# Experts of a mixture-of-experts stage: the smallest one moves from last to third, a 32-slot group becomes 32 extra columns, another group is finished after the last tile

## The chip, the cores and the metric

The kernel runs on one core of a Trainium2 chip. The metric is the device time of one execution in microseconds (us), as the median of several runs. The engines are TensorE (PE for matmuls, PEld for its weight loads), VectorE (DVE), ScalarE (ACT), GpSimd (POOL) and SyncE (SP). Here SP issues the loads of the weights, and POOL issues the indirect transfers that gather rows of tokens from the output tensor and scatter results back.

## The reference, cut to what matters

```python
def _attn_ref(q, k, v, centroids):                 # 4 batches, 8 heads, 768 tokens, 64 wide
    q_assign = argmax(q_n . c_n); k_assign = argmax(k_n . c_n)      # 16 clusters per head
    scores = where(q_assign == k_assign, q . k / 8, -1e9)
    return softmax(scores) . v

def _moe_ref(x, w_skip, w_gate, w1, w2):           # x: 3072 tokens of 512; 8 experts, 1024 hidden
    do_compute = x @ w_skip > 0
    e_idx, gate_w = argmax and softmax weight of (x @ w_gate)
    for e in range(E):
        h = maximum(x[mask] @ w1[e], 0.0)
        y[mask] = gate_w[mask, None] * (h @ w2[e])
    out[do_compute] = x + y                        # the other tokens keep x
```

## The kernel before, in words

The attention takes the first 440 us or so and writes x to the output tensor; the expert stage, which the change touches, works on that tensor in place. Expert 0 is computed beside the end of the attention. The seven others stand at positions p = 1 to 7 of the loop at the end of `experts` (from L1711). Position 1 is the fullest expert known before the last batch, and positions 2 to 7 are the rest by falling number of tokens; `positions` finds which expert that is, at run time. `SHAPE[p]` says how many slots a position has: so many tiles of 128 tokens, and groups of 32 for what goes beyond. Before: position 1 has 256 slots, position 2 has 256 + 32 (group 0, the far group), position 3 has 128 + 64 (groups 1, 2), positions 4 to 6 have 128 + 32 (groups 3, 4, 5), position 7 has 128.

Products are made of float32 numbers split into a high and a low part (`split` for weights, `turned` for rows, which are transposed on TensorE first), three matmuls for each (`three`). There are three ways through an expert:

- A full expert (256 slots): `hidden` keeps the weights as stationary operand and moves 256 columns of tokens, 96 matmuls; `result` then does the second layer for each tile of 128 tokens, 24 matmuls of 512 columns each.
- A light expert (128 slots): `hidden_rows` moves 512 columns of weights, 24 matmuls; its result goes to SBUF (`HS`), is transposed and split (`turn`), and `second_layer` is 24 more.
- A group of 32 slots: it works in plain float32 on the unsplit weights. `group_turn` transposes its rows, `group_hidden` (L1636) makes 16 matmuls of 256 columns, `group_back` (L1646) transposes the result with two, `group_result` (L1655) makes 32 matmuls of 128 columns. `group_hidden` and `group_back` run one position ahead of `group_result`, which stands at the head of its own position.

All results end in `mix` (L1178, x + gate * y, DVE) and `scatter` (L1328, POOL). `gather` is L1321. A scatter writes the output tensor that a gather reads, so a gather that is queued behind scatters waits for them to land, and a scatter behind gathers waits for those. POOL takes its queue in order. `gathers(p + 2)` fetches the rows of the position after the next one, `group_gathers` those of the groups; the places of the groups come from `group_lists` (far group) and `group_places` (others), both in position 1.

The weights come in pieces of 512 KB through eight buffers (`wraw`); `ahead` asks for the next four, and a piece can be loaded once the buffer's old piece has been split and, where a group reads it, used by `group_hidden` or `group_result`. The split (L1552 on ACT for the high part, L1553 on DVE for the low part) goes into one set of tiles for w1 and one for w2, so the split for p + 1 trails the last matmuls of p.

The order of instructions on each engine comes from the framework's scheduler, which starts from the order of the code; `overflow_table` (DVE, a table for tokens beyond all slots; the loop at the very end runs zero times on this input) is spread between other work.

## Time and profile before

| | |
|---|---|
| median of 3 runs (lowest, highest) | 596.77 us (596.75, 597.57) |
| the profiled execution: its own time | 597.92 us |
| its span, first to last instruction | 596.2 us |
| PE busy | 578.9 us (97%) |
| DVE, ACT, POOL busy | 486.9 (82%), 390.6 (66%), 358.6 (60%) us |
| last matmul ends at | 587.8 us |

The times of the trace are microseconds from the start of the span. Positions 1 to 7 run from about 452 us to the end. In the timeline a row gives the start, the duration, the engine and line, what is written from what, how many instructions were merged into the row, and in square brackets how long the engine was idle before it and what released it. A plain float32 matmul leaves two records.

### The profile page before, as it was taken

The page shows a single profiled execution, that of the slowest core. Times are in us where ns is not written, and L with a number is a line of the kernel's source. Part 1 is how long each engine was busy: PE and PEld are TensorE (multiplying, and loading weights), DVE is VectorE, ACT ScalarE, POOL GpSimd, SP SyncE. Part 2 cuts the span into 40 slices and gives each one's busy share as a digit, 9 for nine tenths or more (in the row PEclk, how much of TensorE's full clock was granted, in tenths as well). Part 3 has the DMA queues.
Part 4 walks back from the last instruction along what each step waited for, and adds up shares of the span by engine and source line. Part 5 has one row for each costly group of instructions (what it writes and reads, how often), then busy time and mean ns, then how long its engine had stood idle before and what let it go on. Part 6 is the DMA issues. An engine that isn't in the chain of part 4 may idle for free.

```text
span 596.2 us, 12896 instructions
## 1 busy us (share of the span) xinstructions
PE 578.9 (97%) x4118; PEld 416.6 (70%) x4118; DVE 486.9 (82%) x1032; ACT 390.6 (66%) x917; POOL 358.6 (60%) x391
## 2 busy tenths in 40 slices
PE   7899999999999999999999999999999999999994
PEld 2566667777677766777676776665589787777773
DVE  7987698897989997899997897888569985666781
ACT  7467768677767875778667775975346525566670
POOL 8976859688868877688867686753023230323210
PEclk9999999999999999999999999999999999999998
DMA  7396696766856876668676694765133694598730
GB/s 221 85 235 145 168 216 151 172 152 170 197 140 169 205 177 163 159 154 205 165 159 164 183 221 113 220 185 167 30 125 126 235 320 142 201 305 292 269 123 19
DMA packets 52517, 105.05 MB, mean 176 GB/s; under 512 B 8395, under 2 KB 22777, under 8 KB 52448
## 3 DMA queue, kind: packets, MB, share of 16 engines
q1 hardware_dynamic: 49904, 97.81, 60.7%
q0 software_dynamic: 2144, 6.19, 2.9%
q8 instruction: 34, 0.56, 0.4%
q14 instruction: 35, 0.29, 0.2%
q10 hardware_dynamic: 400, 0.20, 0.1%
HBM read 55.76 MB, written 9.57 MB: 110 GB/s over the span
## 4 chain that ended last, share of the span: by engine, by line
PE 84%; DVE 6%; issue 4%; DMA 2%; POOL 1%; ACT 1%; SPq 1%; POOLq 0%; ACTq 0%; DVEq 0%
PE ps L718 21%; PE ps L692 12%; PE ps L633 11%; PE ps L693 11%; PE ps L1139 4%; PE ps L1140 4%; PE ps L1141 4%; PE ps L748 2%; PE ps L538 2%; PE ps L807 2%; PE ps L1158 2%; PE ps L1655 2%; PE ps L1161 2%; PE ps L1162 2%; PE ps L1636 2%
## 5 line engine op out<-in xcount | busy, mean ns | idle before, releaser
L635 DVE TENSOR_REDUCE M<-ps 128x1 f32<-128x512 f32 (+1 forms) x374 | 190.9, 551 | 41.8 <-PE ps L633 38.3
L707 POOL TENSOR_TENSOR acc<-acc,PT 128x384 f32<-128x384 f32 x134 | 123.5, 950 | 42.9 <-ACT PT L695 39.7
L692 PE MATMUL ps<-D 98*128 98x384 f32 x384 | 134.9, 351 | 2.6 <-DVE M L635 2.4
L707 POOL TENSOR_TENSOR acc<-acc,wraw 128x384 f32<-128x384 f32 x112 | 112.0, 1031 | 31.4 <-ACT wraw L695 25.9
L633 PE MATMUL ps<-D 96*128 96x512 f32 (+1 forms) x374 | 129.0, 348 | 1.8 <-ACT D L600 1.7
L693 PE MATMUL ps<-D 128*128 128x384 f32 x384 | 130.0, 339 | 0.0
L695 ACT ACTIVATE PT<-ps 128x384 f32<-128x384 f32 x216 | 98.7, 495 | 39.4 <-PE ps L693 32.7
L695 ACT ACTIVATE wraw<-ps 128x384 f32<-128x384 f32 x168 | 77.9, 494 | 16.0 <-PE ps L693 6.5
L692 PEld LDWEIGHTS ps<-D 98*128 98x128 f32 x384 | 72.8, 190 | 19.7 <-issue 6.4
L633 PEld LDWEIGHTS ps<-D 96*128 96x128 f32 x374 | 70.7, 190 | 13.8 <-issue 5.8
L693 PEld LDWEIGHTS ps<-D 128*128 128x128 f32 x384 | 73.1, 190 | 7.5
L718 PE MATMUL ps<-PT,vt 128*64 128x385 f32 x432 | 75.4, 492 | 0.0
L718 PE MATMUL ps<-wraw,vt 128*64 128x385 f32 x336 | 57.9, 492 | 0.0
L718 PEld LDWEIGHTS ps<-PT,vt 128*64 128x64 f32 x432 | 28.8, 136 | 34.8 <-issue 33.9
L1552 ACT ACTIVATE D<-wraw 128x1024 fp32r<-128x1024 f32 (+1 forms) x45 | 43.9, 1009 | 8.8 <-PE ps L1141 7.0
L1328 POOL DMA_INDIRECT out<-yo,ixw x7 | 11.1, 1583 | 54.9 <-DVE yo L1178 49.2
L718 PEld LDWEIGHTS ps<-wraw,vt 128*64 128x64 f32 x336 | 22.7, 137 | 27.4 <-issue 26.1
L489 DVE TENSOR_TENSOR raw<-raw,D 128x768 fp32r<-128x768 f32 x28 | 41.7, 1501 | 0.0
L701 POOL TENSOR_TENSOR acc<-PT 128x384 f32<-128x384 f32 x36 | 30.7, 872 | 14.6 <-ACT PT L695 14.5
L1553 DVE TENSOR_TENSOR D<-wraw,D 128x1024 fp32r<-128x1024 f32 (+1 forms) x29 | 33.9, 1182 | 5.5 <-ACT D L1552 5.4
L829 ACT ACTIVATE x<-ps,rs 128x64 f32<-128x64 f32 x162 | 35.3, 307 | 2.7 <-DVE rs L760 1.2
L701 POOL TENSOR_TENSOR acc<-wraw 128x384 f32<-128x384 f32 x28 | 28.0, 1020 | 5.9 <-ACT wraw L695 5.9
(377 smaller groups left out, 1033.6 us busy)
## 6 DMA issues: line engine op xcount, KB each, us to landing
wraw<-w SPq DMA_DIRECT2D x64, 512.0 KB
D<-D SPq DMA_DIRECT2D x124, 192.0 KB
raw<-qk SPq DMA_DIRECT2D x16, 768.0 KB
D<-raw SPq DMA_DIRECT2D x60, 192.0 KB
vt<-v SPq DMA_DIRECT2D x16, 384.0 KB
out<-x SPq DMA_DIRECT2D x31, 192.0 KB
D<-mk SPq DMA_DIRECT2D x120, 24.0 KB
D<-mr SPq DMA_DIRECT2D x56, 1.5 KB
```

What stands on the lines that cost most here:

```text
L489: eng.tensor_tensor(out=lo.bitcast(F32R), in0=lo, in1=c[f"hi{t}"].bitcast(F32), op=ALU.subtract)
L633: nc.tensor.matmul(sm, lhsT=c["qm"][a][0:96, j * P:(j + 1) * P], rhs=c["kb"][a][0:96, m0:m1], start=True, stop=True)
L635: nc.vector.tensor_reduce(out=c["m"][:, j, a, hf:hf + 1], in_=sm, axis=AX.X, op=ALU.max)
L692: nc.tensor.matmul(ps, lhsT=c["kb"][a][0:98, ks], rhs=c["qm"][a][0:98, sl], start=True, stop=False)
L693: nc.tensor.matmul(ps, lhsT=c["kc"][a][:, ks], rhs=c["qc"][a][:, sl], start=False, stop=True)
L695: nc.scalar.activation(out=pt, in_=ps, func=AF.Exp, scale=D ** -0.5)
L701: nc.gpsimd.tensor_tensor(out=acc, in0=self.pt(i, s - 2)[:, :HALF], in1=pt, op=ALU.add)
L707: (nc.vector if dve else nc.gpsimd).tensor_tensor(out=acc, in0=acc, in1=pt, op=ALU.add)
L718: nc.tensor.matmul(av[a * D:(a + 1) * D, :], lhsT=c["vt"][:, kt, a * D:(a + 1) * D], rhs=self.pt(i, hf * 2 * KT + kt * 2 + a), start=(kt = ...
L829: self.nc.scalar.activation(out=c["x"][:, j, cs], in_=xp[:, n, cs], func=AF.Copy, scale=c["rs"][:, j, 2 * hp + a:2 * hp + a + 1])
L1552: nc.scalar.activation(out=h[:, cs], in_=r[:, cs], func=AF.Copy)
L1553: nc.vector.tensor_tensor(out=l[:, cs], in0=r[:, cs], in1=h.bitcast(F32)[:, cs], op=ALU.subtract)
```

## The change

It does five things. (1) The order of positions: the least loaded expert moves from position 7 to position 2, and ranks 2 to 6 move back by one (`RANKS`, `SHAPE`, and the `ranks` tile that `positions` compares with). (2) The far group, now at position 3, goes through `hidden` as 32 more columns (288 in place of 256); its `group_hidden` and `group_back` go, its rows are transposed in `prepare`, the Relu of its columns is copied once more in float32 (`hg`), and `group_result` runs after the first two of eight steps of the first `result`. (3) At position 7 `group_result` runs after the last `finish`. (4) `overflow_table` runs at position 3 in place of 2. (5) In position 1 only the far group is gathered; groups 1 and 2 are gathered in position 2.

```diff
-SHAPE = {1: (2, ()), 2: (2, (0,)), 3: (1, (1, 2)), 4: (1, (3,)), 5: (1, (4,)), 6: (1, (5,)), 7: (1, ())}
+SHAPE = {1: (2, ()), 2: (1, ()), 3: (2, (0,)), 4: (1, (1, 2)), 5: (1, (3,)), 6: (1, (4,)), 7: (1, (5,))}
+RANKS = (0, 1, 7, 2, 3, 4, 5, 6)
...
         def prepare(p):
...
+            w = wide(p)
+            hi, lo = (xp.tile([P, KD, CAP + OT], F32R, name=f"x{n}{c}", bufs=1)[:, :, :w] for c in "hl")
+            for k in range(KD):
+                tp = bank()
+                for j in range(n):
+                    nc.tensor.transpose(out=tp[:, j * P:(j + 1) * P], in_=x[:, j, k * P:(k + 1) * P], identity=self.ident)
+                both(hi[:, k, :CAP], lo[:, k, :CAP], tp)
+            if w > CAP:
+                tp = psum("tp", P)
+                nc.tensor.transpose(out=tp, in_=self.XG[SHAPE[p][1][0]], identity=self.ident)
+                both(hi[:, :, CAP:], lo[:, :, CAP:], tp.rearrange("p (k t) -> p k t", t=OT))
...
+        def hidden(xh, xl, w1h, w1l, w):
...
             for f in range(KF):
-                ph = psum("ph", CAP)
+                ph = psum("ph", w)
...
+                if w > CAP:
+                    nc.scalar.activation(out=hg[f], in_=ph[:, CAP:], func=AF.Relu)
...
             for f in range(KF):
                 cs = slice(f % 2 * DM, (f % 2 + 1) * DM)
                 three(py, hh[:, f, js], hl[:, f, js], w2h[f // 2][:, cs], w2l[f // 2][:, cs], f == 0, f == KF - 1)
+                if between and f == 1:
+                    between()
...
-            for g in mine:
-                group_result(backs[g], self.halves[p, 1], self.XG[g], *groups[g][1:])
             if tiles == CT:
-                h = hidden(*xs, *w1s)
-            else:
+                *h, hg = hidden(*xs, *w1s, wide(p))
+                backs.update((g, hg) for g in mine)
+
+            def group_results():
+                for g in mine:
+                    group_result(backs[g], self.halves[p, 1], self.XG[g], *groups[g][1:])
+                if tiles == CT:
+                    ahead(2 * p + 4)
+
+            if tiles < CT:
+                if p < E - 1:
+                    group_results()
...
                 groups = {0: group_lists(group_rows(far))}
-                group_gathers(2)
+                group_gathers(3)
                 groups.update(self.group_places(pm, psum, ot))
-                group_gathers(3)
                 self.hold(n0, mark)
             elif p + 2 < E:
                 group_gathers(p + 2)
-            if p == 2:
+            if p == 3:
                 self.overflow_table(ot)
...
                 finish(py, rows(p)[:, 0, :], idx[:, :1], gate[:, :1])
+                if p == E - 1:
+                    group_results()
```

Two places show what it moves. In the names, `yo` is a finished tile, `oyo` a finished group, `xg0` to `xg2` are rows of tokens, `idro` and `idrg` the places of the far group and of the others in the gather's list, and a wait on `DMASW` is one for an indirect transfer to land.

POOL, from the gather of the far group in position 1 on, before:

```order
L1321 DMA PT_65<-out,idro_5512 128x128 [waits DVE_49]
L1321 DMA PT_65<-out,idrg_5535 128x128 [waits DVE_49]
L1321 DMA PT_65<-out,idrg_5535 128x128
L1328 DMA out<-yo_5583,idw_4980 3072x512 [waits DMASW3_49,DMASW2_49,DMASW6_49,DMASW1_49,DMASW7_49,DMASW0_49,DVE_49]
L1328 DMA out<-yo_5663,idw_4980 3072x512 [waits DVE_49]
L1328 DMA out<-oyo_5700,idwo_5513 12288x128 [waits DVE_49]
L1321 DMA xg1_5137<-out,ixr_5307 128x512 [waits DMASW5_49,DMASW6_49,DMASW4_49,PE_49]
```

The same place after (lines are four higher):

```order
L1325 DMA PT_65<-out,idro_5507 128x128 [waits DVE_49]
L1332 DMA out<-yo_5580,idw_4983 3072x512 [waits DMASW6_49,DMASW1_49,DMASW7_49,DMASW0_49,DVE_49]
L1332 DMA out<-yo_5625,idw_4983 3072x512 [waits DVE_49]
L1325 DMA xg1_5140<-out,ixr_5310 128x512 [waits DMASW3_49,DMASW2_49,PE_49]
L1325 DMA PT_65<-out,idrg_5530 128x128 x2
L1332 DMA out<-yo_5761,ixw_5311 3072x512 [waits DMASW5_49,DMASW6_49,DMASW4_49,DVE_49]
```

The two gathers of groups 1 and 2 (`idrg`) stood ahead of the two scatters of position 1 and now stand behind them, and behind the gather of the rows of position 4 (`xg1`), which waits for both scatters to land.

PE, the end of position 2 and the first matmuls of position 3, after (L1143 to L1145 are `three`, L1579 the far group's transpose in `prepare`, L1657 `group_turn`, L1153 `turned`):

```order
L1143 MATMUL ps_88<-D_64 128x512
L1579 MATMUL ps_88<-ident_101,PT_65 128x128 [waits DVE_49]
L1144 MATMUL ps_88<-vtW_4787,D_64 128x512
L1145 MATMUL ps_88<-vtW_4787,D_64 128x512
L1657 MATMUL ps_88<-ident_101,PT_65 128x128 [waits DMASW5_49,DVE_49]
L1657 MATMUL ps_88<-ident_101,PT_65 128x128 [waits DMASW6_49,DVE_49]
L1153 MATMUL ps_88<-ident_101,xg1_5140 128x128 [waits DMASW4_49,Activation_49]
L1143 MATMUL ps_88<-x2l_5729,D_64 128x288 [waits DVE_49]
```

And the place where before the same two transposes of groups 1 and 2 stand, between the last matmul of the hidden layer of position 2 and the first of its second layer:

```order
L1140 MATMUL ps_88<-x2h_5617,rawW_4493 128x256
L1141 MATMUL ps_88<-x2h_5617,D_64 128x256
L1627 MATMUL ps_88<-ident_101,PT_65 128x128 [waits DMASW2_49]
L1627 MATMUL ps_88<-ident_101,PT_65 128x128 [waits DMASW3_49]
L1139 MATMUL ps_88<-D_64,hh_5705 128x512 [waits Activation_49]
```

The two transposes and one of position 4's, each with a wait for a gather, now stand ahead of the hidden layer of position 3.

## Rows read from the trace of the kernel before

**Rows 1.** The page: busy time, share of the span and instructions of TensorE and its neighbours.
```profile
PE 578.9 (97%) x4118; PEld 416.6 (70%) x4118; DVE 486.9 (82%) x1032; ACT 390.6 (66%) x917; POOL 358.6 (60%) x391
```
**Rows 2.** Timeline of PE, end of position 1 and the far group in position 2.
```profile
474.61 0.47 PE L1141 MATMUL ps<-vtW,hl 128*128 128x512 f32 x1
...
475.25 1.93 PE L1636 MATMUL ps<-wraw,oxt 128*32 128x256 f32 x32
...
477.69 0.44 PE L1646 MATMUL ps<-ident,ohs 128*128 128x128 f32 x2
...
478.60 1.51 PE L1655 MATMUL ps<-wraw,oht 128*32 128x128 f32 x46
...
481.63 0.39 PE L1139 MATMUL ps<-x2l,D 128*128 128x256 f32 x1
```
**Rows 3.** Timeline of PE, from the end of position 2's hidden layer to position 3.
```profile
492.17 0.28 PE L1141 MATMUL ps<-x2h,D 128*128 128x256 f32 x1
...
508.18 3.83 PE L1655 MATMUL ps<-wraw,oht 128*32 128x128 f32 x128
511.94 0.50 PE L1158 MATMUL ps<-rawW,D 128*128 128x512 f32 x1
```
**Rows 4.** Timeline of PE, positions 6 and 7: first matmuls of a hidden layer, last matmul.
```profile
562.57 0.50 PE L1158 MATMUL ps<-rawW,D 128*128 128x512 f32 x1
...
573.11 0.50 PE L1158 MATMUL ps<-rawW,D 128*128 128x512 f32 x1 [0.21 <-ACT D L1151]
...
575.94 0.39 PE L1161 MATMUL ps<-D 128*128 128x512 f32 x1
...
587.45 0.39 PE L1141 MATMUL ps<-vtW,D 128*128 128x512 f32 x1
```
**Rows 5.** Timeline of POOL: gathers and scatters, with the idle time before.
```profile
471.33 1.00 POOL L1321 DMA_INDIRECT PT<-out,idro  x1 [10.11 <-DVE idrg L1344]
...
473.94 1.70 POOL L1321 DMA_INDIRECT PT<-out,idrg  x1 [0.30 <-issue]
478.24 1.02 POOL L1328 DMA_INDIRECT out<-yo,idw  x1 [2.61 <-DVE D L1553]
479.57 1.02 POOL L1328 DMA_INDIRECT out<-yo,idw  x1 [0.30 <-issue]
...
513.51 0.98 POOL L1328 DMA_INDIRECT out<-oyo,idwg  x1 [0.30 <-DVE oyo L1178]
519.88 2.06 POOL L1321 DMA_INDIRECT xg<-out,ixr  x1 [5.39 <-DMA out<-oyo,idwg]
...
562.75 1.74 POOL L1328 DMA_INDIRECT out<-yo,ixw  x1 [5.93 <-DVE yo L1178]
...
588.90 0.98 POOL L1328 DMA_INDIRECT out<-yo,ixw  x1 [8.78 <-DVE yo L1178]
```
**Rows 6.** Indirect transfers, 420 to 597 us: count, median us from issue to landing.
```profile
xg<-out,ixr POOLq DMA_INDIRECT x7, 6.3
...
PT<-out,idrg POOLq DMA_INDIRECT x5, 3.3
...
out<-yo,idw POOLq DMA_INDIRECT x2, 7.6
```
**Rows 7.** The same of single transfers: issued at 513.51, 577.27 and 489.60.
```profile
out<-oyo,idwg POOLq DMA_INDIRECT x1, 5.5
out<-yo,ixw POOLq DMA_INDIRECT x1, 4.6
xg<-out,ixr POOLq DMA_INDIRECT x1, 3.4
```
**Rows 8.** Timeline of DVE: a mix, a low part of rows, a low part of weights.
```profile
475.15 0.74 DVE L1178 SCALAR_TENSOR_TENSOR yo<-ps,gate1t,xg 128x512 f32<-128x512 f32 x1
...
478.08 0.42 DVE L1152 TENSOR_TENSOR x2l<-ps,x2h 128x256 fp32r<-128x256 f32 x1
...
562.38 1.21 DVE L1553 TENSOR_TENSOR D<-wraw,vtW 128x1024 fp32r<-128x1024 f32 x1
```

More of the change, by code (lines that the diff above doesn't have):

```diff
@@ L175, in constants @@
         nc.gpsimd.memset(self.place[:, :1], 2.0 ** 17)
+        self.ranks = const.tile([P, E - 2], F32, name="ranks")
+        iota(self.ranks, [[1, E - 2]], base=RANKS[3] - 1)
+        nc.gpsimd.memset(self.ranks[:, :1], float(RANKS[2]))
         self.NG = self.ntok // OT
@@ L1381, in overflow_table @@
         cap = small.tile([P, E], F32, name="ocap")
-        sizes = [CAP // OT] + [tiles * P // OT + len(groups) for tiles, groups in (SHAPE[r] for r in range(1, E))]
+        sizes = [CAP // OT] + [tiles * P // OT + len(groups) for tiles, groups in (SHAPE[RANKS.index(r)] for r in range(1, E))]
         nc.vector.memset(cap, float(sizes[0]))
@@ L1496, in group_places @@
         nc, vec = self.nc, self.nc.vector
-        rs = [r for r in range(3, E) if SHAPE[r][1]]
+        rs = [r for r in range(2, E) if SHAPE[r][0] == 1 and SHAPE[r][1]]
         n, r0 = len(rs), rs[0]
@@ L1561, in prepare, with both, wide @@
             x, n = rows(p), SHAPE[p][0]
-            hi, lo = self.X1 if n == 1 else (xp.tile([P, KD, n * P], F32R, name=f"x{n}{c}", bufs=1) for c in "hl")
-            self.turned([x[:, j, k * P:(k + 1) * P] for k in range(KD) for j in range(n)], hi, lo, bank)
-            return hi, lo
+            if n == 1:
+                hi, lo = self.X1
+                self.turned([x[:, 0, k * P:(k + 1) * P] for k in range(KD)], hi, lo, bank)
+                return hi, lo
+            w = wide(p)
[9 more added lines that the diff above has]
+                both(hi[:, :, CAP:], lo[:, :, CAP:], tp.rearrange("p (k t) -> p k t", t=OT))
+            return hi, lo
+        def both(hi, lo, x):
+            nc.scalar.activation(out=hi, in_=x, func=AF.Copy)
+            nc.vector.tensor_tensor(out=lo, in0=x, in1=hi.bitcast(F32), op=ALU.subtract)
+        def wide(p):
+            return CAP + OT * len(SHAPE[p][1])
         def finish(py, x, idx, gate):
@@ L1570, in finish @@
             scatter(yo, idx)
-        def hidden(xh, xl, w1h, w1l):
-            hh = hp.tile([P, KF, CAP], F32R, name="hh")
-            hl = hp.tile([P, KF, CAP], F32R, name="hl")
+        def hidden(xh, xl, w1h, w1l, w):
+            hh, hl = (hp.tile([P, KF, CAP + OT], F32R, name=f"h{c}") for c in "hl")
+            hg = ot.tile([P, KF // OC, OC, OT], F32, name="oht2", bufs=2) if w > CAP else None
+            if w > CAP:
+                hg = [hg[:, f % (KF // OC), f // (KF // OC), :] for f in range(KF)]
             for f in range(KF):
-                ph = psum("ph", CAP)
+                ph = psum("ph", w)
                 fs = slice(f * P, (f + 1) * P)
@@ L1648, in group_back @@
             nc.scalar.activation(out=ht.rearrange("p m c t -> p m (c t)"), in_=th, func=AF.Copy)
-            return ht
+            return [ht[:, f % (KF // OC), f // (KF // OC), :] for f in range(KF)]
         def group_result(ht, w2, x, oid, og, apart=True):
@@ L1723, in experts @@
             w2s = split(self.halves[p, 1], "w2")
-            ahead(2 * p + 4)
+            if tiles < CT:
+                ahead(2 * p + 4)
             if p + 2 < E:
```

21 lines of the change are left out of this document (11 added, 10 removed).

## The prediction, made before the changed kernel was run

> **What bounds the kernel now.** I read the page first: TensorE is busy for 578.9 of 596.2 us [rows 1]. In the timeline of PE the expert stage runs without a break but for three places: about 1.1 us in the far group's second layer, which takes from 478.60 to 481.63 where two groups later need 511.94 - 508.18 = 3.76, 1.88 each [rows 2, 3]; about 0.5 us between positions 6 and 7, where position 7's first matmul stands alone at 573.11 and the rest follows at 575.94 [rows 4]; and the end. The last matmul starts at 587.45; the last scatter is issued at 588.90 and the span ends at 596.2, 7.3 us later [rows 4, 5]. So the time is the sum of PE's work from position 1 on, its idle gaps, and that tail. I follow PE through the new order, with stage lengths taken from the old one.
>
> **The change part by part.** Position 1 ends on PE at 474.61 + 0.23 = 474.85 [rows 2]. Two transposes fewer (128 rows to prepare, not 256) and the far group's moved away take about 0.3 off: **474.6**.
>
> Position 2 is now light. Three things can set its length.
>
> PE's own work: positions 3 to 5 take (562.57 - 511.94) / 3 = 16.88 each [rows 3, 4]. Take off a group's second layer (1.88), its hidden layer (1.9: 475.25 to about 477.1) and back transposes (0.3) [rows 2], add 0.6 for five more transposes in `prepare` and for those of groups: 13.4, so PE would be through at 488.0. One of these is useless: the far group is still transposed by `group_turn`, about 0.1.
>
> DVE and ACT: position 6, which had no group ahead of it, took 575.94 - 562.57 = 13.4, with PE waiting for ScalarE [rows 4]. Position 2 has five more evacuations, 0.3 to 0.42 each on DVE and as many on ACT [rows 8], some 1.5: 489.5.
>
> POOL: this is the term that I expect to decide. Before, groups 1 and 2 were gathered right behind the far group, 20 us ahead of their use. Now two transposes that wait for these gathers, and one that waits for the rows of position 4, stand on PE ahead of position 3's hidden layer; and the gathers are queued behind the two scatters of position 1, because the gather of position 4's rows waits for these to land. The chain: the far group's gather starts at 471.33 as before [rows 5] and lands some 3.1 later (3.3 is the median of its kind [rows 6]). The next issue starts 0.85 after a landing: 513.51 + 5.5 = 519.0, and the gather that waited for it starts at 519.88 [rows 5, 7]. So the first scatter starts at 475.3, the second at 476.6 (its mix, 475.15 + 0.74 - 0.3, is over by then [rows 8]; issue to issue is 1.33 [rows 5]). It lands 7.6 later [rows 6], at 484.2; position 4's gather starts at 485.05, the two of the groups at 486.55 and 487.85. The last lands 3.3 later, position 4's rows 6.3 after their issue [rows 6]: 491.15 and 491.35. With 0.85 to be seen, position 3's hidden layer starts at **492.2**, 4.2 after PE would be free. The bounds: with the shortest landings in the trace, 4.6 for a scatter with the DMA idle, 3.4 for a gather [rows 7], the chain is over by 488.3, and DVE and ACT set 489.5. With issues of 1.74 in place of 1.0, as one at 562.75 took [rows 5], and longer landings the start goes to 496. I take the medians, since weight loads fill the DMA engines in this stretch, before and after.
>
> The page "DMA: Bandwidth & Descriptors" of the Trainium skill (section "Anatomy of one DMA — SWDGE (gpsimd) path") gives 2.0 us plus bytes over 436e3 for such a transfer, some 2.6 us for a scatter of 262 KB, an estimate. By that the chain would be over before 486 and the first rival below would hold; the rows show 7.6 for both scatters of position 1 [rows 6], so the trace disagrees beside weight loads.
>
> Position 3, hidden layer: 88 matmuls of 256 columns start between 481.63 and 492.17, 0.121 apart [rows 2, 3]. One of 512 columns takes 0.23: 47 starts from 575.94 to 587.45, less eight transposes at about 0.11 [rows 4]. Between the two, 288 columns take 0.135: 96 x 0.135 = 13.0 (11.6 if the 32 columns cost nothing). To 505.2. The eight extra small Relus on ACT and the table on DVE, some 7 us of small operations, lie beside these 13 us; DVE had room for the table beside 11.6 before.
>
> The rest of position 3: 492.17 to 508.18 was 16.0 [rows 3]; 0.12 of it is the last hidden matmul, 0.3 are the transposes that moved, and the far group's second layer adds 1.9: 17.5, to 522.7. I count the 1.1 us of idle time as gone, since nothing in the trace holds that work where it now stands; kept, it is 1.1 more. The w2 buffers are now held until there, so the loads for position 4 start some 14 us before their first use at 522.7. That covers them. SP's load of the loop count stands ahead of them; the table is finished by then.
>
> Two groups' second layer, 3.76 [rows 3]: 526.5. Positions 4 and 5: 16.88 each, 560.2. Position 6, whose successor's group is finished late: 16.88 - 1.88 = 15.0, 575.2; the 0.5 us of idle time ahead of a position with no group is inside position 2 now. Position 7: from 575.94 to 587.45, plus its last matmul and the one done early, 0.23 each: 12.0 [rows 4], 587.2. Its group, 1.9: **589.1**, where before the last matmul ended at 587.7.
>
> The tail: before, a mix of 512 columns (0.74 [rows 8]), then 0.3 to the scatter and 7.3 to the end [rows 5]. Now the large scatter goes out while the group is computed, and a mix of 128 columns, taken as 0.35, ends last: 589.1 + 0.35 + 0.3 + 7.3 = 597.05. A smaller scatter may land sooner, by at most 1.
>
> The constants need two more small POOL instructions at the start, which the first loads hide (0.2 if not); the comparison with `ranks` has the old shape and costs nothing.
>
> **The sum.** 597.05 against 596.2: +0.85. The profiled execution took 597.92, 1.7 more than its span, and is 1.15 above the median of the runs. Carried over, 596.77 + 0.85 = 597.6. In other words: 2.2 of group work, 1.1 and 0.5 of idle time and 0.4 of tail go, and they are paid for by 1.4 of columns and by the new wait of some 4.
>
> **The rivals.** A, the chain is short: scatters and gathers land early enough that DVE and ACT set the start of position 3, 489.5. For it: 4.6 and 3.4 were seen [rows 7]; against it: both scatters at this place took 7.6 [rows 6]. 2.7 less than the forecast: 594.9. All starts up to 491 belong here, so 594.6 to 596.4.
>
> B, slower: POOL's issues are held by VectorE. A scatter's issue at 562.75 took 1.74, beside a split of weights that ran from 562.38 to 563.59, and ended 0.9 behind it; one at 479.57 took 1.02 [rows 5, 8]. The chain has five issues in a row in a stretch in which DVE runs up to eight such splits. Each held one adds 0.75 to the start of position 3. From one held on the kernel is slower by over 0.2%; with three it is 2.25 more: 599.9. The Trainium skill ("SBUF — State Buffer", section "Who interferes with whom") says that a VectorE instruction with two SBUF inputs blocks a GpSimd one that reads SBUF until it ends; the row at 562.75 agrees.
>
> C, the far group's second layer idles again wherever it stands: 1.1 more, 598.7. Nothing in the trace names what held it, and that speaks for it a little.
>
> **How the numbers follow.** Forecast 0.45, A 0.32, B 0.15, C 0.08. 0.2%, 1.2 us, is about what a measurement of this kernel can tell from no change; the borders are 595.6 and 598.0. A is faster in 0.25 and the same in 0.07. The forecast reaches from 596.4 to 599.2 by the spread of landings; 0.26 of it are below 598.0 and 0.19 above. B and C are slower. So faster 0.25, same 0.33, slower 0.42. The range goes from the middle of A, 594.9, to a little past B's 599.9, 600.2: some 0.1 is left out below and 0.08 above. The forecast's own range is 596.4 to 599.2.
>
> **What would show it.** In the timeline of PE, position 1 should end near 474.6, and a gap of 2 to 5 us stand ahead of the first matmul of 288 columns, at about 492, with three transposes in or behind it; the waits should name a gather (the `idrg` or `xg` transfers on POOL). If the gap is missing, or ends with ScalarE or VectorE, A holds. The 96 matmuls of 288 columns should be 0.135 apart; the far group's 32 matmuls should take 1.9, and the last 32 after 587. The forecast falls if position 3 waits for weights, or if the end is more than 8 us behind the last matmul.

## The result, and the profile after

The changed kernel takes 604.94 us (median of 6 runs, 603.78 to 606.84), and the kernel before 597.17 us beside it (6 runs, 596.5 to 598.4). The ratio is 1.0133, with a 95% interval of 1.0113 to 1.0153. The forecast was 597.6 us, with a range of 594.9 to 600.2 us. So the change costs 7.8 us where 0.8 us was expected, and the time lies outside the range.

The traced execution took 606.15 us with a span of 604.4 us. Its page answers [rows 1]:

```profile
PE 581.3 (96%) x4085; PEld 420.0 (69%) x4085; DVE 485.6 (80%) x1033; ACT 391.3 (65%) x924; POOL 360.4 (60%) x393
```

TensorE's busy time rose by 2.4 us although it has less to do, and the rest of the loss is idle time. The waits of PE name it. The columns are: in all, times, longest. The row had no counterpart before.

```profile
PE ps L1657 <- DMA PT<-out,idrg: 7.2, 2, 6.2
```

L1657 is the transpose in `group_turn`, and idrg are the gathers of groups 1 and 2. The timeline of PE shows where these transposes stand, and what comes of it (start, duration, operation, and in brackets the idle time before):

```profile
475.36 0.39 PE L1162 MATMUL ps<-rawW,D 128*128 128x512 f32 x1
...
488.71 0.40 PE L1145 MATMUL ps<-vtW,D 128*128 128x512 f32 x1
495.34 0.45 PE L1657 MATMUL ps<-ident,PT 128*128 128x128 f32 x1 [6.24 <-DMA PT<-out,idrg]
496.78 0.45 PE L1657 MATMUL ps<-ident,PT 128*128 128x128 f32 x1 [0.99 <-DMA PT<-out,idrg]
497.02 0.42 PE L1153 MATMUL ps<-ident,xg 128*128 128x128 f32 x1
497.09 0.59 PE L1143 MATMUL ps<-x2l,D 128*128 128x288 f32 x1
...
512.31 0.40 PE L1143 MATMUL ps<-D,hh 128*128 128x512 f32 x1
...
513.79 2.26 PE L1685 MATMUL ps<-wraw,oht 128*32 128x128 f32 x64
...
534.17 0.50 PE L1162 MATMUL ps<-rawW,D 128*128 128x512 f32 x1
...
567.86 0.50 PE L1162 MATMUL ps<-rawW,D 128*128 128x512 f32 x1
...
582.76 0.39 PE L1162 MATMUL ps<-rawW,D 128*128 128x512 f32 x1
...
594.79 1.96 PE L1685 MATMUL ps<-wraw,oht 128*32 128x128 f32 x64
```

Position 2 starts at 475.36 and TensorE is through with it at 489. Three transposes hold it until 497.09, where the first matmul of 288 columns starts. Position 3's first layer then takes 15.22 us, to 512.31, and not 13.0. The stages of two us tell why (PE busy and instructions, granted clock as a share of full speed, share of the DMA engines, GB/s):

```profile
488.00:490.00 2.00, 1.10 (x6) 1.00 1.03 420
490.00:492.00 2.00, 0.00 (x0) 1.00 0.91 330
492.00:494.00 2.00, 0.00 (x0) 0.53 0.17 68
494.00:496.00 2.00, 0.45 (x1) 0.50 0.20 59
496.00:498.00 2.00, 1.22 (x6) 0.50 0.02 6
498.00:500.00 2.00, 2.00 (x10) 0.50 0.31 117
500.00:502.00 2.00, 2.00 (x10) 0.50 0.04 8
502.00:504.00 2.00, 2.00 (x16) 0.91 0.43 131
```

Some 3 us into the idle time the granted clock falls to 0.50, which is 1.2 of 2.4 GHz, and it comes back at about 502.3. At half clock 10 matmuls fit into 2 us, at full clock 17.

What released TensorE so late stands in the chain of work that ended last, which was made of matmuls here before:

```profile
472.07 1.00 DMA PT<-out,idro
...
479.03 0.38 POOL out L1332
...
481.11 7.57 DMA out<-yo,idw
...
489.51 0.38 POOL xg L1325
...
490.88 2.79 POOL PT L1325
...
493.97 2.68 DMA PT<-out,idrg
496.78 0.45 PE ps L1657
```

Read downwards: the far group's gather (idro) is issued at 472.07 and lands 6.1 us later (indirect transfers issued from 472 to 474: count, median us from issue to landing):

```profile
PT<-out,idro POOLq DMA_INDIRECT x1, 6.1
```

The first scatter of position 1 waits for this landing and starts at 479.03; the second starts at 481.11 and lands 7.57 later. The gather of position 4's rows starts at 489.51, and the two gathers of groups 1 and 2 follow, the first with an issue of 2.79 us. The last landing lets TensorE go. This is the chain of the prediction, link for link; only its lengths are others.

| step | predicted | trace after | later by |
|---|---|---|---|
| position 1 ends on PE | 474.6 | 475.36 | 0.8 |
| first scatter of position 1 issued | 475.3 | 479.03 | 3.7 |
| gather of position 4's rows issued | 485.05 | 489.51 | 4.5 |
| second gather of idrg issued | 487.85 | 493.97 | 6.1 |
| first layer of position 3 starts | 492.2 | 497.09 | 4.9 |
| first layer of position 3 ends | 505.2 | 512.31 | 7.1 |
| two groups done | 526.5 | 534.17 | 7.7 |
| position 6 starts | 560.2 | 567.86 | 7.7 |
| the last group starts | 587.2 | 594.79 | 7.6 |
| end of the span | 597.05 | 604.4 | 7.35 |

Of the 7.7 us that are lost when the two groups are done, 7.1 are lost by 512; the rest of position 3 then takes 0.6 more than predicted, and from there on the stages have the predicted lengths.

### The profile page after: what moved, and what is told of

It reads as the page before. It is cut to its first block, busy times and chain, and to the rows that moved or that the text cites. A ratio compares the mean times of both kernels' runs of the same rounds, so it can differ in the third digit from the quotient of the medians.

```text
span 604.4 us, 12832 instructions
## 1 busy us (share of the span) xinstructions
PE 581.3 (96%) x4085; PEld 420.0 (69%) x4085; DVE 485.6 (80%) x1033; ACT 391.3 (65%) x924; POOL 360.4 (60%) x393
## 5 line engine op out<-in xcount | busy, mean ns | idle before, releaser
L711 POOL TENSOR_TENSOR acc<-acc,wraw 128x384 f32<-128x384 f32 x112 | 114.1, 1049 | 29.6 <-ACT wraw L699 24.0
L493 DVE TENSOR_TENSOR raw<-raw,D 128x768 fp32r<-128x768 f32 x28 | 37.6, 1353 | 0.0
L1332 POOL DMA_INDIRECT out<-yo,ixw x7 | 9.2, 1316 | 47.2 <-DVE yo L1182 36.9
```

Source lines behind the costliest of these rows:

```text
L493: eng.tensor_tensor(out=lo.bitcast(F32R), in0=lo, in1=c[f"hi{t}"].bitcast(F32), op=ALU.subtract)
L711: (nc.vector if dve else nc.gpsimd).tensor_tensor(out=acc, in0=acc, in1=pt, op=ALU.add)
```

## The experiments

**Theory T:** the loss is TensorE's wait for late landings ahead of position 3, because transposes that need them stand first in its queue, and the half clock behind that wait. **Rivals:** something else would hold position 3 anyway; the landings are slow because the weights are now loaded beside them; the wide columns or the reordering cost time by themselves.

**The transposes moved back (e1_pin).** On TensorE alone, the turns of groups 1 and 2 and of position 4's rows are tied behind the last matmul of position 3's first layer (`newest_pe` returns the TensorE instruction written last).

```diff
                 *h, hg = hidden(*xs, *w1s, wide(p))
+                hidden_end = self.newest_pe()
...
+                    n1 = self.written()
                     turned.update((g, group_turn(self.XG[g])) for g in SHAPE[p + 1][1])
+                    if p == 3:
+                        self.hold(n1, hidden_end)
...
+                        n1 = self.written()
                         group_first(p + 1)
                         ahead(2 * p + 5)
                         xs = prepare(p + 1)
                         group_middle(p + 1)
+                        if p == 3:
+                            self.hold(n1, hidden_end)
```

> The changed kernel with one thing different: on TensorE the turns of groups 1 and 2 and of position 4's rows stand behind position 3's first layer instead of ahead of it; the POOL queue is as it was. Theory T (TensorE stands 6.2 + 1.0 us ahead of position 3 only because three transposes of late landings stand first in its queue, and loses about 2.4 us more by the half clock that follows): the first layer of position 3 starts at about 490.0 instead of 497.1 and takes 12.8 instead of 15.2 us, so 604.9 - 9.5 = 595.4 us, and the waits on the gathers vanish from TensorE. Rival S (something else, such as the splits of the weights or of the wide rows, holds position 3 anyway): it starts at 493 or later, 599 to 602 us. Rival K (the clock falls there without the idle time): about 597.8 us.

Measured: 596.49 us, ratio to before 0.9991 (0.9982 to 1.0001). The gathers still come after position 3 has started, the last idrg being issued at 490.38 (at 493.58 in e1_again, the same kernel once more, against 493.97 in the changed kernel), but nobody waits for them. The timeline of PE and the stages:

```profile
489.45 0.40 PE L1146 MATMUL ps<-x2l,D 128*128 128x288 f32 x1 [0.81 <-DVE x2l L1588]
...
502.49 0.48 PE L1146 MATMUL ps<-D,hh 128*128 128x512 f32 x1
```

```profile
492.00:494.00 2.00, 2.00 (x17) 1.00 0.09 23
```

Position 3 starts at 489.45, and its first layer takes 13.04 us at full clock. T holds, S and K fall: against the changed kernel's 604.94 us, 8.4 us go with the place of a few transposes, where T said 9.5. The 0.81 us that are left are VectorE's.

**The gathers moved ahead (e2_gathers_first).** TensorE's order stays; the gathers of groups 1 and 2 and of position 4's rows (into the unused half of position 2's buffer) are issued ahead of position 1's scatters.

```diff
         def rows(p):
+            if p == 4:
+                return xg[2][:, 1:, :]
...
-            if p + 2 < E:
+            if p + 2 < E and p != 2:
                 gathers(p + 2)
             if p == 1:
+                gathers(4)
...
                 groups.update(self.group_places(pm, psum, ot))
+                group_gathers(4)
...
-            elif p + 2 < E:
+            elif p + 2 < E and p != 2:
                 group_gathers(p + 2)
```

> The changed kernel with the gathers of groups 1 and 2 and of position 4's rows (into the free half of position 2's buffer) issued ahead of position 1's two scatters; TensorE's order is as it was. Theory T (the POOL chain makes the landings late): idrg issue at about 473.4 and 474.7 and land by 481, the scatters start at about 482 and land by 490.5, position 2's mix may wait up to 1 us for its buffer, and position 3 starts at about 490: 595.4 to 596.5 us. Rival Q (landings are slow because of the weight loads, wherever the gathers stand in the queue): the transposes still wait for the gathers and the time stays above 600. Rival B (the scatters, now later, become the wait, through the two yo buffers): a wait of 2 us or more on a scatter ahead of position 3, 597 to 600 us.

Measured: 597.00 us, 0.9993 (0.9983 to 1.0002). The wait for gathers is gone; a shorter one is left, for a copy on ScalarE that the next transpose needs:

```profile
PE ps L1153 <- ACT oxt L1659: 1.1, 1, 1.1
```

T holds from its other end, 0.5 us above its range: moving either the landings or their readers is enough. Q and B fall, though the scatters were now issued as late as 482.62 and 484.97.

**The wait filled with work (e3_fill).** 48 matmuls of 288 columns, whose sums nothing reads, stand where TensorE waited; the turns of groups 1 and 2 are tied behind them.

```diff
+            if p == 3:
+                n1, last = self.written(), self.newest_pe()
+                ps = psum("ph", 288)
+                for n in range(48):
+                    nc.tensor.matmul(ps, lhsT=xs[0][:, 0, :P], rhs=xs[0][:, 0, :], start=(n == 0), stop=(n == 47))
+                self.hold(n1, last)
+                filled = self.newest_pe()
...
+                n1 = self.written()
                 *h, hg = hidden(*xs, *w1s, wide(p))
...
+                if p == 3:
+                    self.hold(n1, filled)
...
+                    n1 = self.written()
                     turned.update((g, group_turn(self.XG[g])) for g in SHAPE[p + 1][1])
+                    if p == 3:
+                        self.hold(n1, filled)
```

> The changed kernel with TensorE's wait replaced by useless work of about the same length: 48 matmuls of 288 columns (48 x 0.133 = 6.4 us, their sums are not read) between position 2 and position 3, and the turns of groups 1 and 2 behind position 3's first layer. Theory T (the idle time, not the delay itself, takes TensorE's clock to half): position 3's first layer starts at about 496.3 and runs at full clock, 12.8 us instead of 15.2: about 601.7 us. Rival K (the clock falls there for another reason): granted clock about 0.5 again for some 10 us, 604 us.

Measured: 603.45 us, 1.0101 (1.0084 to 1.0118), 1.7 us more than T said; 0.7 of these lie in the tail, where the span ends 10.35 us behind the start of the last group, against 9.61 in the changed kernel. The timeline of PE and the stages:

```profile
489.26 6.59 PE L1750 MATMUL ps<-x2h 128*128 128x288 f32 x48
495.68 0.29 PE L1146 MATMUL ps<-x2l,D 128*128 128x288 f32 x1
...
508.61 0.48 PE L1146 MATMUL ps<-D,hh 128*128 128x512 f32 x1
```

```profile
496.00:498.00 2.00, 2.00 (x17) 1.00 0.07 23
```

The clock stays whole, and the first layer takes 12.93 us, 495.68 to 508.61, against 15.22. So the idle time took the clock and K falls: 2.3 us of the loss are the clock, the rest is the wait itself. The fill, 6.42 us, is nearly as long a delay as the wait was, 7.2 us; e1_pin has neither.

**The weights held back (e4_loads_late).** Why does idro take 6.1 us to land, and not the 3.1 of the prediction? Position 3's first weights are now loaded beside it. Before, their buffers were held until the far group's own first layer, L1636, had read them, as the waits of SP's queue from 465 to 480 say. The waits of before, then the issues of loads on this queue, of before and of after:

```profile
SPq L1439 <- PE ps L1636: 13.7, 2, 13.5
```

```profile
475.95 2.11 SPq L1439 DMA_DIRECT2D wraw<-w  x4
```

```profile
469.40 1.62 SPq L1443 DMA_DIRECT2D wraw<-w  x2
```

With them the DMA engines' busy share from 470 to 474 is 1.05, against 0.18 before (stages of before and of after: busy time of PE, PEld, DVE, ACT and POOL, granted clock, DMA share, GB/s):

```profile
470.00:474.00 4.00, 4.00 (x22) 3.29 (x22) 3.20 (x18) 2.87 (x5) 2.06 (x3) 1.00 0.18 58
```

```profile
470.00:474.00 4.00, 4.00 (x22) 3.09 (x22) 2.77 (x17) 2.77 (x4) 1.00 (x1) 1.00 1.05 407
```

The experiment holds these two loads behind a small load that reads what idro brought.

```diff
                 group_gathers(3)
+                seen = ot.tile([1, 8], F32, name="seen")
+                nc.sync.dma_start(out=seen, in_=self.XG[0][:1, :8])
+                seen = self.newest()
...
+                        if p == 1:
+                            self.load_pieces(24, 26)
+                            n1 = self.written()
+                            self.load_pieces(26, 28)
+                            self.hold(n1, seen)
+                        else:
+                            ahead(2 * p + 5)
-                        ahead(2 * p + 5)
```

> The changed kernel with the last two of the four loads of position 3's first weights held back until the far group's gather (idro) has landed, by a small load of the gathered rows ahead of them in SP's queue. Theory L (idro took 6.1 us instead of 3.1 because weights of position 3 now load beside it): idro lands in about 3.1 us, the chain of scatters and gathers behind it comes 3 us sooner, TensorE's wait ahead of position 3 falls from 6.2 to about 3.2 us, 600 to 602 us. Rival M (the landing is slow for another reason, for example the loads that were already under way): idro again about 6 us, 604.5 to 606 us.

Measured: 605.71 us, 1.0133 (1.0112 to 1.0154). The indirect transfers in the trace (count, median us from issue to landing), from 472 to 474, from 477 to 481.5 and from 488.5 to 491.6:

```profile
PT<-out,idro POOLq DMA_INDIRECT x1, 3.7
...
out<-yo,idw POOLq DMA_INDIRECT x2, 8.3
...
PT<-out,idrg POOLq DMA_INDIRECT x2, 5.5
```

L is right about the landing, which falls from 6.1 to 3.7, and wrong about the time. The loads now run beside the two scatters, which land in 8.3 instead of 7.5 us and whose issues take 1.93 and 1.95 us. Even so the second idrg is issued at 491.44, 2.5 us sooner than in the changed kernel. But the DMA engines are still full then (share 1.03 from 492 to 494, against 0.17), and the two idrg land in 5.5 us each, against 4.3 and 2.7. The first lets TensorE go at 495.76, in the changed kernel at 495.34, and the waits for the two are 5.7 us. The weights have to be moved somewhere in this stretch; in this run the scatters and the last gathers paid for what idro was spared.

**Only the groups' gathers moved ahead (e5_groups_first).** The two edits of e2_gathers_first that concern groups, without those for position 4's rows.

```diff
                 groups.update(self.group_places(pm, psum, ot))
+                group_gathers(4)
...
-            elif p + 2 < E:
+            elif p + 2 < E and p != 2:
                 group_gathers(p + 2)
```

> The changed kernel with only the gathers of groups 1 and 2 ahead of position 1's scatters; the gather of position 4's rows stays behind them, and the first transpose of those rows stays ahead of position 3's first layer on TensorE. Theory T (what stands first in TensorE's queue and last in POOL's chain makes the wait, whichever rows they are): the wait moves from the groups to position 4's rows: scatters start at about 482.6 and 485, land by 491 to 492, the gather is issued at about 492 and lands at 495 to 496, TensorE waits about 6 us with half clock behind it: 602.5 to 604.5 us. Rival G (only the groups' gathers, which VectorE's splits held up, cost the time): position 3 starts by 491, 597 to 598 us.

Measured: 604.71 us, 1.0134 (1.0115 to 1.0153). The waits of PE:

```profile
PE ps L1153 <- DMA xg<-out,ixr: 6.9, 1, 6.9
```

T holds, 0.2 us above its range, and G falls: one transpose of position 4's rows, now the last link of the chain, costs as much as all three did. Moving two of the three gathers won nothing.

**VectorE's splits held back (e6_splits_later, e6_again, after_again, after_third, e6_third).** In the changed kernel the issue of the first idrg took 2.79 us beside two splits on VectorE (timeline of DVE):

```profile
490.44 1.21 DVE L1557 TENSOR_TENSOR D<-wraw,D 128x1024 fp32r<-128x1024 f32 x1
491.57 1.21 DVE L1557 TENSOR_TENSOR D<-wraw,vtW 128x1024 fp32r<-128x1024 f32 x1
```

It ended at 493.67, 0.9 behind the second split. Tied behind the first result of position 3's first layer, these splits, and the small operations for the overflow, leave VectorE idle here.

```diff
+                n1 = self.written()
                 *h, hg = hidden(*xs, *w1s, wide(p))
+                hidden_dve = next(i for i in list(self.nc.cur_bb.bb.instructions)[n1:] if i.engine == mybir.EngineType.DVE)
...
+            n1 = self.written()
             w2s = split(self.halves[p, 1], "w2")
+            if p == 3:
+                self.hold(n1, hidden_dve)
...
+                n1 = self.written()
                 self.overflow_table(ot)
+                self.hold(n1, hidden_dve)
```

> The changed kernel (turns of groups 1 and 2 ahead of position 3 as it has them) with VectorE's splits of position 3's second weights and the table of the overflow held back behind the first result of position 3's first layer, so that VectorE is idle while POOL issues the gathers. Theory H (POOL's issue of the first idrg took 2.79 instead of 1.0 us, and the first scatter 1.77, because VectorE's splits, which read two operands in SBUF, held it): both idrg are issued in 1.0 us, the last lands about 1.8 us sooner, TensorE waits 1.8 us less, 602.5 to 603.2 us. Rival N (the issue was long for another reason): 2 us or more again, 604.9 us.

Measured: 606.96 us (604.42 to 608.83), 1.0151 (1.0122 to 1.0181), no better than the changed kernel. But its trace, at 604.42 us, has both issues short (timeline of POOL), and a wait of 4.3 us instead of 7.2:

```profile
489.09 1.01 POOL L1325 DMA_INDIRECT PT<-out,idrg  x1 [0.31 <-issue]
490.40 1.00 POOL L1325 DMA_INDIRECT PT<-out,idrg  x1 [0.30 <-issue]
```

The trace said H and the median said N, so I took more pairs of a time and a trace, first one of each kernel.

> The kernel of e6_splits_later once more, for one more pair of a time and a trace. If the spread of its times (604.4 to 608.8 us) is the length of the half clock behind TensorE's wait, which was 3.4 us in its one trace at 604.4 us, then a time above 606 us goes with a longer stretch (about 10 us, as in the changed kernel's trace), and a time near 604.4 with 3.4 us again. Rival: times above 606 us with the same 3.4 us stretch.

> The changed kernel once more, for one more pair of a time and a trace. If the length of the half clock sets where in 603.8 to 606.8 us an execution lies: 10.2 us of half clock behind the wait goes with about 606 us, 3.4 us with about 603.5 us. Rival: no such pairing.

Measured: 600.92 us for e6_again and 607.22 us for after_again. The half clock lasted about 3.4 us in both traces of e6, at 604.42 and at 600.92 us, and about 10 us in after_again as in the first trace of the changed kernel. So its length does not set by itself where an execution lies; in the trace at 604.42 a later wait of 1.1 us for a copy on ScalarE is a part of the difference. Then both kernels on one chip, with more times.

> The changed kernel on the same chip as the three below, as their measure: 604 to 606 us beside 597 for before, with one more trace: TensorE waits 6 to 7.5 us ahead of position 3 and the first idrg is issued in over 2.5 us.

> The kernel of e6_splits_later with more times, beside the changed kernel on one chip. Theory H (the held issues are 2 to 3 us of the loss): both traces so far have the wait at 4.2 to 4.3 us instead of 7.2, so the median of many lies 2.5 to 4 us under the changed kernel's, 601 to 602.5 us. Rival N (what is taken from the issues comes back elsewhere, as three of five times so far, 606.3 to 608.8 us, suggest): the medians are within 0.6 us of each other or e6 is slower.

Measured: 605.98 us for after_third, 1.0149 (1.0136 to 1.0162), and 603.25 us for e6_third, 1.0107 (1.0089 to 1.0124). The waits of PE, of after_third and then of e6_third:

```profile
PE ps L1657 <- DMA PT<-out,idrg: 5.9, 2, 4.0
```

```profile
PE ps L1657 <- DMA PT<-out,idrg: 5.3, 2, 4.5
```

In after_third's trace it was the second idrg that was held, 2.72 us, and the first took 1.01; in e6_third's both took 1.0. On this chip the edit is worth 2.7 us, so H holds there and N falls. But the wait fell only by 0.6 us between these two traces. Another 1.1 us are the first layer, 14.21 us (495.44 to 509.65) against 15.34 (496.48 to 511.82), with 6.8 instead of 10 us at half clock. So 2.7 us is the price of the whole edit on one chip, not of the held issues alone, and the first scatter's issue, 1.70 us in e6_third, was not freed by it. Why e6_splits_later came out at 606.96 us on its chip stays open.

**The far group as a group again (f1_no_wide, e1_again, f1_again).** On top of e1_pin, `wide` returns `CAP`, and the far group takes the way of the other groups.

```diff
         def wide(p):
-            return CAP + OT * len(SHAPE[p][1])
+            return CAP
...
-            for g in SHAPE[p][1] if SHAPE[p][0] == 1 else ():
+            for g in SHAPE[p][1]:
                 inner[g] = group_hidden(turned.get(g) or group_turn(self.XG[g]), self.halves[p, 0])
...
-            for g in SHAPE[p][1] if SHAPE[p][0] == 1 else ():
+            for g in SHAPE[p][1]:
                 backs[g] = group_back(inner[g])
...
-                backs.update((g, hg) for g in mine)
```

> The kernel of e1_pin with the far group computed as a group again (its own transposes, 64 moving passes for the first layer and the turn back) instead of as 32 more columns of position 3. By the steps measured in the trace (288 against 256 columns: 0.133 against 0.12 us a step, 96 steps, 1.3 us; the group's first layer and turn back 2.2 to 2.4 us), the wide columns are worth about 1 us: 597.5 us here against 596.5 for e1_pin. Rival: the group's work falls into time in which TensorE waits anyway (the 0.8 us for the last wide rows), then no difference, 596.5 us.

Measured: 597.72 us beside 598.54 for before, 0.9984 (0.9973 to 0.9995). Before took 597.26 us beside e1_pin, so the two can't be compared by their times; e1_pin and this kernel ran again on one chip.

> The kernel of e1_pin beside f1_no_wide on one chip. If the wide columns are worth what their matmuls say (e1_pin 13.04 us for 96 steps against 11.81, and the group's own first layer, turn back and waits 1.6 us less), the two are within 0.6 us of each other, both 0.3 to 1.3 us under before.

> The kernel of f1_no_wide beside e1_pin on one chip: within 0.6 us of it by the traces; if the wide columns are worth the 1 us that the prediction gave them, 0.7 us or more slower.

Measured: 596.49 us for e1_again, 0.9990 (0.9981 to 0.9999), and 597.27 us for f1_again, 1.0005 (0.9996 to 1.0014). By the medians the wide columns are worth 0.8 us. The traces don't show it where the sum put it: from the start of position 2 to the end of position 3's first layer f1_again needs 27.05 us (475.49 to 502.54) and e1_again 27.62 (474.93 to 502.55), so the 1.23 us by which 96 wide steps are longer (13.04 us in e1_pin against 11.81) and the 0.82 us that e1_again waits for its last wide rows cost at least as much as the group's own first layer. What makes f1_again longer in its trace is the end, 9.0 us from the last matmul's start at 586.71 against 8.0, with no change of code there. The gain of the columns is small, and its place is open.

**The last group ahead of position 7 (f2_no_end).** On top of e1_pin, `group_results()` is called for position 7 where it is for the others.

```diff
-                if p < E - 1:
-                    group_results()
+                group_results()
...
-                if p == E - 1:
-                    group_results()
```

> The kernel of e1_pin with the last group's second layer ahead of position 7's layers again, not at the very end. The work on TensorE is the same. If the group at the very end gains by leaving a smaller last scatter (landing 2.2 us for the group's rows against 3.3 for the full tile) and costs its own 1.9 us behind the tile, the two are within 0.7 us: 596.5 to 597.2 us. Rival: the end of the kernel is set by the last landing alone, whatever its size, then 596.5 us as e1_pin.

Measured: 597.71 us beside 598.54, 0.9989 (0.9978 to 0.9999), beside e1_pin's 0.9991 on another chip. Where this group stands makes no difference that these runs show.

**The last 0.8 us (f3_best).** e1_pin with the edit of e6_splits_later, and without the far group's useless turn.

```diff
-                    turned.update((g, group_turn(self.XG[g])) for g in SHAPE[p + 1][1])
+                    turned.update((g, group_turn(self.XG[g])) for g in SHAPE[p + 1][1] if SHAPE[p + 1][0] == 1)
```

> The kernel of e1_pin, without the turn of the far group that nothing reads (0.1 us), and with VectorE's splits of position 3's second weights and the table of the overflow behind the first result of position 3's first layer. Theory: in e1_pin position 3 waits 0.81 us for the last wide rows, which stand on VectorE behind one such split; without it the first layer starts about 0.9 us sooner: 595.6 us, ratio to before 0.997. Rival: the splits that are moved back make the second layer of position 3 wait (four of 1.2 us beside eight results of 0.45), 596.5 us or more.

Measured: 598.71 us beside 598.54, 1.0005 (0.9993 to 1.0017). Position 3 did start sooner, at 488.58 against 489.45 in e1_pin, and had given it back by 520.75, where the two groups of position 4 begin (at 520.52 in e1_pin). The waits of PE name most of it:

```profile
PE ps L1679 <- ACT ohs L1673: 0.9, 1, 0.9
```

The groups' transposes wait for a copy on ScalarE, for which e1_pin does not wait. The rival was right about the time, not about the place. The larger part of what this trace has over e1_pin's lies in the tail, though: the span ends 11.7 us behind the start of the last group, against 9.7, with no change of code there, and that is open.

**The columns without the new order (g1_wide_only).** `SHAPE` and `RANKS` as before, with the far group as columns of position 2; the gathers of groups 1 and 2 and `overflow_table` go back to where they stood before, too.

```diff
-SHAPE = {1: (2, ()), 2: (1, ()), 3: (2, (0,)), 4: (1, (1, 2)), 5: (1, (3,)), 6: (1, (4,)), 7: (1, (5,))}
-RANKS = (0, 1, 7, 2, 3, 4, 5, 6)
+SHAPE = {1: (2, ()), 2: (2, (0,)), 3: (1, (1, 2)), 4: (1, (3,)), 5: (1, (4,)), 6: (1, (5,)), 7: (1, ())}
+RANKS = (0, 1, 2, 3, 4, 5, 6, 7)
...
+                group_gathers(2)
+                groups.update(self.group_places(pm, psum, ot))
                 group_gathers(3)
-                groups.update(self.group_places(pm, psum, ot))
...
-            if p == 3:
+            if p == 2:
                 self.overflow_table(ot)
```

> The order of the kernel before (the least loaded expert last) with the far group as 32 more columns of position 2, so that one part of the change stands alone. Theory T: TensorE is through with position 1 at about 474.6 and the turns of the far group and of groups 1 and 2 now stand ahead of position 2's first layer, while their gathers, issued from 471.3 on, land at 474.5 to 481: TensorE waits 5 to 7 us, its clock may fall behind that (0 to 2.6 us), and the wide columns give back about 1 us: 601 to 606 us. Rival V (only the far group's own landing counts, 3.1 us): a wait of 1 to 2 us, 597 to 599 us.

Measured: 603.08 us beside 596.80, 1.0092 (1.0071 to 1.0113). The timeline of PE and the stages:

```profile
480.61 0.30 PE L1579 MATMUL ps<-ident,PT 128*128 128x128 f32 x1 [2.50 <-DMA PT<-out,idro]
...
481.61 0.61 PE L1143 MATMUL ps<-x2l,D 128*128 128x288 f32 x1
```

```profile
482.00:484.00 2.00, 2.00 (x10) 0.50 0.30 115
```

The time is T's, the wait is V's. A wait of 2.5 us for idro, a stage that begins some 3 us later in this trace (its idro is issued at 474.70), and a first layer of 14.39 us at partly half clock make the 6 us (why the stage begins later was not taken apart); T's 5 to 7 us of waiting were not there, since both idrg had landed too. So the light expert in between seems to be what gives the far group's gather its time; it is the next gathers that it leaves too little.

## Why the prediction was wrong

**What held.** The place and the name of the new wait: a gap ahead of the first matmul of 288 columns, with the three transposes behind it and `idrg` as the releaser. The stage lengths: 96 wide steps in 13.04 us when the clock is whole (predicted 13.0), the rest of position 3 in 18.03 (17.5; e1_pin, 502.49 to 520.52), two groups in 3.74 (3.76), positions 4 and 5 in 16.85 each (16.88), position 6 in 14.90 (15.0), position 7 in 12.03 (12.0), the tail behind the last matmul 7.65 (7.95). The far group's second layer takes 2.19, 0.3 more than the two-group rows said (1.88, as they said, in e1_pin), so rival C's 1.1 us of idle time did not come back. Rival A's start, 489.5 if the chain were no bound, is what e1_pin shows: 489.45. And no position waits for weights.

**Step one: idro "lands some 3.1 later".** It took 6.1. The step took the usual landing of such a gather [rows 6], and the stretch seemed to bear that out, with a DMA share of 0.18 before. It took the loads to be the same before and after, and did not ask what the change does to them: without the far group's reading of position 2's first weights, buffers come free sooner and the next loads meet the gather. The prediction looked at these buffers only for position 4's loads. e4_loads_late shows that the loads are the cause, and that holding these two back only moved the price.

**Step two: issues of 1.0 us.** In the trace the first scatter took 1.77 and the first idrg 2.79, 2.6 us more for the two. That is rival B's mechanism, at a chance of 0.15 and 0.75 us for each; a held issue can cost more than twice that when two splits follow one another. The trace of before had such a case, in the scatter at 577.27, whose landing the prediction used [rows 7] (timeline of POOL):

```profile
577.27 2.85 POOL L1328 DMA_INDIRECT out<-yo,ixw  x1 [11.50 <-DVE yo L1178]
```

VectorE split weights from 576.91 to 579.27, and the issue ended 0.85 behind that. e6_third prices the idrg's part, with what came of it for the clock, at 2.7 us. The section "Who interferes with whom" of "SBUF — State Buffer" in the Trainium skill, that a VectorE instruction with two SBUF inputs blocks a GpSimd one that reads SBUF until it ends, agrees with these rows but for the 0.9 us between the end of the split and that of the issue; where it infers that `tensor_tensor` leaves the generation of descriptors alone, the rows go against it.

**Step three: the clock was no term at all.** A wait of 4.2 us was written into the sum at its own length. With 6.2 us of idle time TensorE came back at 1.2 GHz, and the first layer took 15.22 us instead of 12.93 (e3_fill). That is 2.3 us, a third as much as the wait.

**In the other direction** went the 0.85 us between a landing and TensorE's start, which is 0.1 here, and the last landing, 2.7 instead of 3.3. The start, 0.8 later in this trace, is no term: over the traces of the changed kernel and its variants with this order position 2 starts anywhere from 474.60 to 476.33.

**Carrying over.** The sum was made against an execution 1.15 us above the median of its runs, and 1.15 was taken off. e1_pin's span, 594.6, is within 0.3 of what the sum gives for A (597.05 - 2.7 = 594.35), but its time is 596.49, not 594.9: its trace is 0.1 under its own median. That suggests that the extra time of the traced execution of before lay somewhere that the sum never used, and should not have been taken off; one trace does not show it. Without it A would have been "the same", not "faster".

**The terms together.** 597.6 + 3.0 (landing) + 2.6 (issues) + 2.3 (clock) - 0.7 and - 0.6 (the quicker start and the shorter last landing) make 604.2, against 604.94 measured; the 0.7 us between them was not taken apart. The range had no room for these terms together. The prediction's own late bound for the start of position 3, 496, gives 597.6 + 3.8 = 601.4, yet the range ends at 600.2; the start came at 497.09, and the clock was in neither. That the terms came together is no accident, as far as the traces go: a shorter position 2 brings the loads, the splits and the gathers into the same 20 us.

The fastest kernel that was measured is e1_pin, 1.4 to 1.6% under the changed kernel. Against the kernel before it gains some 0.1%: 0.9991 (0.9982 to 1.0001) and 0.9990 (0.9981 to 0.9999) in two comparisons, the first of which includes no gain.

## What to carry to other kernels

When a change shortens a stage, list what its length used to hide, queue by queue: here position 2 went from 37 us [rows 2, 3] to 14, the gathers, scatters and loads under it lost their cover, and the loss, 7.8 us, was more than ten times the 0.1% that e1_pin's order gains. Look at what stands first in an in-order queue, not only at what is needed first: three small transposes that were not needed for another 20 us held 96 matmuls, and tying them behind these gave the loss back. And price a wait of TensorE of several us with the half clock that follows it.

## What the runs showed of the hardware that was not expected

- In the first trace of the changed kernel TensorE's granted clock fell to 0.50 (1.2 GHz) 3.0 us after the last matmul, while it was still idle. In the other traces with such a wait it fell from 0.8 (e4_loads_late) to 4.8 us (e6_splits_later) after it; in e6_splits_later and g1_wide_only TensorE had just begun to work again. It stayed low for about 10 us in all three traces of the changed kernel, whose waits were 5.9 to 7.3 us, though from 497 on TensorE was busy without a break. It was about 7 us in e5_groups_first, 3.4 us in g1_wide_only, and 3.4, 3.4 and 6.8 us in the traces of e6. What sets the length stays open.
- The landings of indirect transfers differed far more with what else was moved than with their size: 6.1 us for the 64 KB of idro beside weight loads and 3.7 us with two of these loads held back (e4_loads_late); 6.2 to 8.3 us (medians of two) for position 1's scatters of 256 KB beside weight loads and 2.7 us for the same two in g1_wide_only, where the DMA engines' share was 0.30 to 0.36; 3.3 us for one of that size at the quiet end of the kernel, where the 64 KB of the last group took 2.2. "DMA: Bandwidth & Descriptors" of the Trainium skill (section "Anatomy of one DMA — SWDGE (gpsimd) path") has 2.0 us plus bytes over 436e3, some 2.6 us for the scatter, an estimate. The quiet end comes near it, the loaded stretches don't.
- An issue on POOL that usually takes 1.0 us took up to 3.13 us (e5_groups_first, at 489.85) while VectorE split weights.
